# Attention and gated MLP on one core: a gather taken earlier in the gate, and a measurement of weights made one projection later

## The chip, the cores and the metric

The kernel runs on one core of a Trainium2 chip. The core's engines work side by side and are tied together by semaphores: TensorE (matrix products, which it writes to PSUM), VectorE, ScalarE, GpSimd, and SyncE, which only issues DMAs. In the profile they are called PE, DVE, ACT, POOL and SP; PEld is TensorE's loading of weights, and a name with q is the engine's queue. Each engine executes its own instructions in the order in which they were written. The metric is the device time of one execution in microseconds (us), lower is better.

## The reference, cut to what matters

The inputs are `x` (1 × 2048 × 512) and weights, all float32. Two blocks follow each other, each with a normalisation ahead and the input added behind:

```python
h  = x + attention(layernorm(x))        # 32 heads of 16, softmax over all 2048 keys, then @ wo
z  = gelu(layernorm(h) @ w_in)          # 2048 x 1376
z1 = z[:, :688]
z2 = layernorm(z[:, 688:])
g  = w_sp @ z2 + b_sp[:, None]          # w_sp is 2048 x 2048: it mixes the positions
h2 = h + (z1 * g) @ w_out               # what is returned
```

## The kernel before, in words

Every product of float32 numbers is made of three products of 16-bit numbers. Each operand is scaled by a power of two and split into a high and a low part, and `mm3` (L107 to L109) adds high × high, high × low and low × high in one PSUM accumulator. The scales are found on the chip, from the weights themselves.

The work has four stages: a prologue that normalises `x` and makes queries, keys and values (span to about 162 us); attention (to about 1295 us); a middle stage with `wo` and `w_in` (to about 1460 us); and the gate with `w_sp` and `w_out`. In all four the order on each engine is written out by hand (`tc.manual_schedule`): an instruction stands in its engine's queue where the Python code emits it. So the place of a line in the code is the place in five queues at once, and an instruction that waits holds up everything that was emitted after it for the same engine.

**Prologue.** The 512 columns of queries and of keys come in four blocks `b` of 128. For each block, `load_wqk(b)` reads the weights, `weigh_wqk(b)` takes the largest magnitude of each row of both (VectorE, L352) and spreads it over a diagonal matrix `each` (GpSimd, L356). The measurement proper, `measure(b, each)`, multiplies a matrix of ones with `each` on TensorE (L374), so that all partitions hold the maxima, and VectorE reduces them (L376) and makes powers of two of them (L299, L300, L302, L378). `weigh_wqk` doesn't call it, it appends it to the list `measures`, and the main code pops it later. `put_wqk(b)` then scales and splits the weights on GpSimd (L366, L100, L104). `proj` and `proj_qk` are the projections: 12 matmuls in four groups `d`; between the groups stand calls of `between(d)`, which take over the result of the projection before (`takes`: ScalarE L458, VectorE L461, or L492 for values), and, for the first two blocks of keys, two copies by ScalarE for sums of keys (L472, L473). There are three accumulators for projections. The measurement of the fourth block stood behind `proj(proj_v, 15)`, the last projection of values. Then a loop over `j` makes the 24 projections of blocks 1 to 3; from `j` = 2 on, `ahead` puts products for the row maxima of the scores among them (L223 on TensorE, L228 on VectorE). `put_wqk(2)` stands at `j` = 1, `put_wqk(3)` at `j` = 8. The last results are taken over by VectorE (L460, L461), then attention begins (L1112).

**Gate.** `w_sp` is taken as 2 × 2 blocks, with Strassen-like sums of blocks that were prepared before, so that seven block products take the place of eight. The loop over `p` handles a pair of row blocks, `p` and `p + 8`, eight times. `product(acc, b)` is one such product, 24 matmuls of 344 columns, and a `ring` of nine tiles brings the operands by DMA. The seven go to three accumulators A, C and B in the order `b11`, `t1`, `t2`, `b22`, `t3`, `b21`, `n4`. The results times `z1` are the tile `now.pr`: `right` (L1504 VectorE, L1505 GpSimd), `br` (L1512, L1513), `left` (L1522, L1523) and `bl` (L1540). Its columns are dealt with in two halves, 1 and 0. `level(half)` finds a power of two for each row (VectorE L1355, L1317 to L1320), `raise_` multiplies with it (ScalarE L1366), `squares` transposes blocks of 32 × 32 on VectorE (L1382 and L1385 for half 1, L1388 for half 0), and after half 0 `send` moves the blocks with 16 DMAs (SP L1395). In the next pair, whose name for this one is `before`, `hi` (ScalarE L1401) and `lo` (VectorE L1410, L1414, L1416) split them, `multiply(half, w)` multiplies them with `w_out` on TensorE, and `gather(half, w, acc)` adds the result to the rows of `h` (VectorE L1455). The accumulators of `multiply` come from the pool `ps_o`, which has two buffers. So `multiply(1, 0)` and `multiply(1, 1)` (8 matmuls of 512 columns each; L107 to L109, L1449, L1450) fill both, and `multiply(0, 0)` and `multiply(0, 1)` (9 matmuls each) need them back from the first and the second gather.

The last pair has no `squares`; its own columns are transposed on TensorE (L1426) instead.

Of the kernel before, what the change touches and what calls it, by code (L numbers as in the profile page):

```python
# [59 lines left out]
def block_kernel(ctx: ExitStack, tc: tile.TileContext, x, wqkv, wo, w_in, w_sp4, b_sp, w_out, out):  # L60
# [194 lines left out]
    def max_rows():  # L255

        g, parts = turned.pop(0)
        t = sm.tile([P, 32], F16, name="mturned")
        nc.vector.transpose(t, parts.rearrange("p t j i -> p (t j i)"))
        nc.sync.dma_start(m_scr[g % 2], t)  # L260
        for j in range(2):
            r0 = RG * j + KS
            nc.sync.dma_start(
                qst[g][r0:r0 + 2].rearrange("r p (c n s) -> r (p c) n s", n=4, s=32),
                m_scr[g % 2].rearrange("(n j r q) s -> j r q n s", n=4, j=2, r=2)[j])
# [3 lines left out]
    with ExitStack() as pre:  # L269
# [244 lines left out]
        kf, accs, rest, measures = {}, [0], [], []  # L514
# [17 lines left out]
        def ahead(k):  # L532
            for _ in range(k):
                m = done[0] // 8
                if not todo and m < LEAD:
                    steps = max_pair(m)
                    todo.extend(steps[i] for i in (0, 1, 4, 2, 5, 3, 6, 7))
                    ends.append(steps[8])
                if todo:
                    todo.pop(0)(done[0] % 5)  # L540
                    done[0] += 1
                    if not todo:
                        ends.pop()()
# [4 lines left out]
        def proj(kind, *which, then=lambda: None, **kw):  # L548

            def between(d):  # L550
                if d == 0 and rest:
                    rest.pop(0)()
                if d == 1:
                    if takes:
                        takes.pop(0)()
                    then()

            takes.append(kind(*which, between, **kw))
# [103 lines left out]
        measures.pop(0)()  # L662
        weigh_wqk(3)
        proj(proj_v, 15)
        measures.pop(0)()

        for j in range(24):
            b, n, i = 1 + j // 8, j // 2 % 4, 1 - j % 2

            def between(d):  # L670
                if d == 1 and j >= FIRST:
                    ahead(5 if j < FIRST + 4 else 4)
                if d == 2 and takes:
                    takes.pop(0)()
                    if rest:
                        rest.pop(0)()
                if d == 3 and turned and done[0] % 8 > 3:
                    max_rows()

            if j in (1, 8):  # L680
                put_wqk(2 + j // 8)
            if j == 3:
                copy_v = load_v(0)
            if j == 7:
                copy_v()
            if j in (8, 12):
                load_q(j // 4 - 1)
            if j == 16:
                fixed(kst[0])
            if j == 20:  # L690
                scales_ = [nc.scalar.alloc_register(f"scale{b}") for b in range(DB)]
                for reg, size in zip(scales_, sizes):
                    nc.scalar.load(reg, size[0:1, 3:4].bitcast(I32))
            takes.append(proj_qk(b, n, i, between))
# [91 lines left out]
    with ExitStack() as at:  # L786
# [13 lines left out]
        def product(s, hg, qb, kb, p, t):  # L800

            r = slice(RG * t, RG * t + KM)
            nc.tensor.matmul(s, kst[hg % 2][r, p, kb * P:(kb + 1) * P],  # L803
                             qst[hg * NQ + qb][r, p, :], start=True, stop=True)
# [484 lines left out]
    with ExitStack() as fin:  # L1289
# [9 lines left out]
        def next_g():  # L1299
            banks[0] += 1  # L1300
            return ps_g[(banks[0] - 1) // 2 % 2].tile([P, 512], F32, name="g")[:, :FC]
# [170 lines left out]
        with tc.manual_schedule(engines={E.PE, E.Activation, E.DVE, E.Pool, E.SP}):  # L1472
            wu = [f1.tile([P, 2 * 3, D], F16, name=f"wu{i}") for i in range(2)]
            raw_w = f1.tile([P, 2 * 3, D], F32, name="raw_w")
            w_top, w_low, w_up, w_down = [f1.tile([P, n], F32, name=f"w_{i}") for i, n in enumerate((6, 1, 1, 1))]
            nc.gpsimd.memset(raw_w[:, 2 * 3 - 1, :], 0.0)
            nc.sync.dma_start(raw_w[:, :5, :], w_out[:5 * P, :].rearrange("(i p) c -> p i c", p=P))
            for r0 in (TW - fn, P - fn):
                nc.sync.dma_start(raw_w[r0:r0 + fn, 5, :], w_out[5 * P:, :])
            nxt = fetch(0)  # L1480
            now = None
            for p in range(HB):
                (z1t, z1b, ht, hb), last = nxt, p + 1 == HB
                nxt = None if last else fetch(p + 1)
                before, now = now, Rows(p, (ht, hb))
                bt, bb = bias_up[:, p:p + 1], bias_up[:, p + HB:p + HB + 1]
                A, C, B = [next_g() for _ in range(3)]
                p1, v, q5 = [f0.tile([P, FC], F32, name=n) for n in ("p1", "v", "q5")]
                left, right = now.pr[:, 0, :FC], now.pr[:, 0, FC:FH]
                bl, br = now.pr[:, 1, :FC], now.pr[:, 1, FC:FH]  # L1490

                product(A, "b11")
                nc.scalar.activation(p1, A, AF.Identity, bias=bt)
                product(C, "t1")
                nc.scalar.activation(q5, C, AF.Identity, bias=bb)
                if not p:
                    weigh_w()
                product(A, "t2", False)
                nc.scalar.activation(v, A, AF.Identity, bias=bt)
                if p:  # L1500
                    before.lower(1, 0, 1)
                    before.lower(0, 0, 1)
                product(C, "b22", False)
                nc.vector.tensor_add(right, C, v)  # L1504
                nc.gpsimd.tensor_mul(right, right, z1t[:, FC:])  # L1505
                if p:
                    before.hi(1)
                    before.hi(0)
                else:
                    measure_w()  # L1510
                product(A, "t3", False)
                nc.vector.tensor_add(br, A, q5)  # L1512
                (nc.vector if last else nc.gpsimd).tensor_mul(br, br, z1b[:, FC:])  # L1513
                if p:
                    before.lo(1)
                    before.lo(0)
                now.level(1, 0, 1)
                now.raise_(1, 0, 1)
                if not last:
                    now.squares(1)  # L1520
                product(B, "b21")
                nc.vector.tensor_add(left, B, p1)  # L1522
                (nc.vector if last else nc.gpsimd).tensor_mul(left, left, z1t[:, :FC])  # L1523
                if p:
                    accs = [before.multiply(1, w) for w in range(2)]
                    for w in range(2):
                        before.gather(1, w, accs[w])
                if last:
                    now.level(0, 0)
                    for w in range(2):  # L1530
                        now.turn(1, w)
                        now.split(1, w)
                    now.lower(1, 0, 1)
                    now.raise_(0, 0)
                if p:
                    accs = [before.multiply(0, w) for w in range(2)]
                    for w in range(2):
                        before.gather(0, w, accs[w])
                product(A, "n4", False)
                nc.vector.scalar_tensor_tensor(bl, A, bb, z1b[:, :FC], op0=ALU.add, op1=ALU.mult)  # L1540
                if p:
                    for w in range(2):
                        before.store(w)
                if last:
                    now.level(0, 1)
                    now.raise_(0, 1)
                else:
                    now.level(0, 0, 1)
                    now.raise_(0, 0, 1)
                    now.squares(0)  # L1550
                    now.send()
            accs = [now.multiply(1, 0)]
            now.turn(0, 0)
            now.split(0, 0)
            accs.append(now.multiply(1, 1))
            now.turn(0, 1)
            now.gather(1, 0, accs[0])
            now.split(0, 1)
            now.gather(1, 1, accs[1])
            now.lower(0, 0, 1)  # L1560
            acc = now.multiply(0, 0)
            now.gather(0, 0, acc)
            now.store(0)
            acc = now.multiply(0, 1)
            for c in (slice(0, D // 2), slice(D // 2, D)):
                now.gather(0, 1, acc, c)
                now.store(1, c)
# [29 lines left out]
```

## Time and profile before

| | |
|---|---|
| median of 3 runs | 1720.6 us (1720.13 to 1721.52) |
| the profiled execution | 1720.39 us |
| its span, first to last instruction | 1718.6 us |
| granted clock of TensorE | 1.00 |
| TensorE busy | 1699.9 us, 99% |
| VectorE busy | 1452.8 us, 85% |
| ScalarE busy | 1317.3 us, 77% |
| GpSimd busy | 813.8 us, 47% |

All times of the trace count from the start of the span. A row of the timeline has the start, the duration, the engine, the line, the operation, output and inputs with their shapes, and how many like instructions are merged in it; in square brackets stands the idle time of the engine just before it and what ended that. A matmul's duration reaches to the end of its write, so that rows of matmuls in a stream overlap: the distance of two starts says how fast TensorE goes. A row of the waits has the instruction that waited, what it waited for, the total in us, how often, and the longest. A row of the chain that ended last has start, duration, engine, tile and line.

### The profile page before, as it was taken

How to read it: one execution, taken by the hardware profiler on the slowest of the kernel's cores; microseconds unless marked ns; L12 is line 12 of the kernel's file. 1: busy time of each engine (PE TensorE's matmuls, PEld its weight loads, DVE VectorE, ACT ScalarE, POOL GpSimd, SP SyncE). 2: the span in 40 equal slices, each digit the busy share in tenths (PEclk: the TensorE clock that was granted, in tenths of full speed). 3: DMA queues.
4: the chain of work that ended last, by engine and by line, in shares of the span. 5: the costliest groups of instructions: out<-in, count | busy, mean ns of one | idle time of the engine just before them, and what ended most of it. 6: DMA issues, size and time to landing. Idle time of an engine off the chain costs nothing.

```text
span 1718.6 us, 36670 instructions
## 1 busy us (share of the span) xinstructions
PE 1699.9 (99%) x13499; PEld 643.9 (37%) x13499; DVE 1452.8 (85%) x3051; ACT 1317.3 (77%) x2584; POOL 813.8 (47%) x1062
## 2 busy tenths in 40 slices
PE   9999999999999999999999999999999999999999
PEld 4533222222222222222222222222225666666655
DVE  7688999999999999999999999999937887533444
ACT  4334999999999999999999999999995554211111
POOL 1231867776673267687677876400002766200100
PEclk9999999999999999999999999999999999999999
DMA  5534332332221244344434444300114454654651
GB/s 183 163 99 134 111 88 64 105 94 81 81 67 25 55 118 117 110 145 123 124 112 139 129 129 126 80 13 19 45 41 125 146 183 143 241 193 159 211 199 44
DMA packets 189309, 196.03 MB, mean 114 GB/s; under 512 B 67496, under 2 KB 140008, under 8 KB 189128
## 3 DMA queue, kind: packets, MB, share of 16 engines
q1 hardware_dynamic: 186824, 188.04, 36.7%
q10 hardware_dynamic: 2304, 5.64, 0.8%
q8 instruction: 106, 1.74, 0.4%
q14 instruction: 75, 0.61, 0.1%
HBM read 122.10 MB, written 65.93 MB: 109 GB/s over the span
## 4 chain that ended last, share of the span: by engine, by line
PE 65%; DVE 16%; DMA 5%; issue 5%; SPq 4%; POOL 3%; ACT 2%; DVEq 0%; ACTq 0%; POOLq 0%
PE pv L828 26%; PE s L803 17%; PE m L223 9%; DVE mx L228 7%; PE acc L107 3%; PE acc L109 3%; PE acc L108 3%; SPq L1395 2%; DMA rc<-r_scr 2%; DVE ab L237 1%; DMA z_scr<-z 1%; DVE og L838 1%; PE g L108 1%; PE g L109 1%; PE g L107 1%
## 5 line engine op out<-in xcount | busy, mean ns | idle before, releaser
L812 ACT ACTIVATE pt<-s 128x512 f32<-128x512 f32 x1968 | 1006.2, 637 | 4.9 <-PE m L223 3.8
L228 DVE TENSOR_REDUCE mx<-m 128x1 f32<-128x512 f32 x1510 | 947.5, 682 | 12.6 <-PE m L223 3.9
L803 PE MATMUL s<-qst,kst 50*128 50x512 f16 x2048 | 604.3, 379 | 0.2
L828 PE MATMUL pv<-pt,vst 128*32 128x256 f32 (+1 forms) x6056 | 598.1, 466 | 4.1 <-DVE og L838 1.3
L223 PE MATMUL m<-kst,qst 48*128 48x512 f16 x1510 | 452.5, 381 | 0.0
L803 PEld LDWEIGHTS <-kst 50*128 50x128 f16 x2048 | 132.0, 94 | 352.0 <-issue 323.7
L828 PEld LDWEIGHTS pv<-pt,vst 128*32 128x32 f32 x6056 | 119.5, 108 | 290.1 <-issue 276.7
L223 PEld LDWEIGHTS <-qst 48*128 48x128 f16 x2048 | 159.1, 93 | 173.7 <-issue 124.3
L223 PE MATMUL m<-uvs,qst 48*128 48x512 f16 x504 | 190.5, 380 | 0.0
L245 POOL TENSOR_SCALAR nm<-nm 128x16 f32<-128x16 f32 x32 | 6.6, 206 | 359.0 <-DVE nm L242 359.0
L237 DVE CUSTOM_DVE_ANT_0 ab<-m,ab 128x512 f32<-128x512 f32 x252 | 170.5, 677 | 2.7 <-ACT ab L233 2.7
L233 ACT ACTIVATE ab<-m 128x512 f32<-128x512 f32 x252 | 157.3, 624 | 16.5 <-PE m L223 15.8
L1366 ACT ACTIVATE pr<-pr,up 128x304 f32<-128x304 f32 (+1 forms) x32 | 17.0, 574 | 114.8 <-DVE up L1320 110.5
L989 POOL TENSOR_TENSOR op<-raw,op 128x512 f16<-128x512 f32 x80 | 92.9, 1161 | 6.0
L912 POOL TENSOR_TENSOR raw<-raw 128x512 f32<-128x512 f32 (+1 forms) x84 | 83.3, 991 | 6.7
L917 POOL TENSOR_TENSOR acc_sp<-acc_sp,raw 128x512 f32<-128x512 f32 x63 | 80.4, 1277 | 4.5
L109 PE MATMUL acc<-wi,hT 128*128 128x344 f16 x256 | 79.1, 309 | 0.3 <-DVE hT L104 0.3
L107 PE MATMUL acc<-wi,hT 128*128 128x344 f16 x256 | 79.1, 309 | 0.0
L108 PE MATMUL acc<-wi,hT 128*128 128x344 f16 x256 | 79.1, 309 | 0.0
L1505 POOL TENSOR_TENSOR pr<-pr,z 128x344 f32<-128x344 f32 x8 | 7.3, 912 | 146.0 <-DMA whole<-squares 110.1
L909 POOL TENSOR_SCALAR raw<-raw 128x512 f32<-128x512 f32 (+1 forms) x88 | 52.3, 594 | 19.7 <-DMA raw<-in_wqkv 12.3
L894 POOL TENSOR_SCALAR raw<-raw,figs 128x512 f32<-128x512 f32 (+1 forms) x84 | 55.8, 668 | 8.8 <-DMA raw<-in_wo 7.9
(247 smaller groups left out, 2238.7 us busy)
## 6 DMA issues: line engine op xcount, KB each, us to landing
raw<-in_w_sp SPq DMA_DIRECT2D x128, 256.0 KB
s_scr<-op SPq DMA_DIRECT2D x64, 256.0 KB
op<-s_scr SPq DMA_DIRECT2D x32, 512.0 KB
a_scr<-op SPq DMA_DIRECT2D x48, 256.0 KB
op<-a_scr SPq DMA_DIRECT2D x24, 512.0 KB
o_scr<-og SPq DMA_DIRECT2D x64, 128.0 KB
qst<-q_scr SPq DMA_DIRECT2D x192, 32.0 KB
kst<-k_scr SPq DMA_DIRECT2D x48, 128.0 KB
```

What stands on the lines that cost most here:

```text
L107: nc.tensor.matmul(ps, lh, rh, start=first, stop=False, **kw)
L108: nc.tensor.matmul(ps, lh, rl, start=False, stop=False, **kw)
L109: nc.tensor.matmul(ps, ll, rh, start=False, stop=last, **kw)
L223: nc.tensor.matmul(acc, q[r, p, c], keys[r, p], start=True, stop=True)
L228: nc.vector.reduce_max(at(t, e if t else e - 1), acc, axis=AX.X)
L233: nc.scalar.activation(ab[0], acc, AF.Abs)
L237: nc.vector.tensor_tensor_reduce(ab[0], acc, ab[0], 0.5, LOW, ALU.add, ALU.max, at(0, 0))
L803: nc.tensor.matmul(s, kst[hg % 2][r, p, kb * P:(kb + 1) * P], qst[hg * NQ + qb][r, p, :], start=True, stop=True)
L812: nc.scalar.activation(pts[p, kb][:, t, :], s, AF.Exp, scale=scales_[hg // 2])
L828: nc.tensor.matmul(pv[0][32 * j:32 * j + 32, a:b], vst[hg % 2][:, c:c + 32], pts[j % 2, kb][:, j // 2, a:b], start=kb == 0, stop=kb == NB - 1,
L912: pool.tensor_mul(got[0] if n else acc, got[0], got[0])
L989: chores.append((lambda: pool.tensor_sub(t[0][:, 1], of(), t[0][:, 0]), TT))
```

## The change

Two edits. In the prologue, the fourth measurement is popped at `j` = 1 of the loop, behind the first of the 24 projections and ahead of `put_wqk(2)`; it stood ahead of that projection. In the gate, for a pair after the first, the two products `multiply(1, 0)` and `multiply(1, 1)` stand directly behind `b21`, and the first gather stands ahead of the sum into `left` (L1522) and of GpSimd's product; the second gather stays behind them. The transposes of half 1 (`now.squares(1)`), which stood ahead of `b21`, stand behind the second gather. TensorE's own order in the gate is the same as before. No instruction is added or taken away.

```diff
@@ prologue @@
         weigh_wqk(3)
         proj(proj_v, 15)
-        measures.pop(0)()
 
         for j in range(24):
...
+            if j == 1:
+                measures.pop(0)()
             if j in (1, 8):
                 put_wqk(2 + j // 8)
@@ gate @@
                 now.level(1, 0, 1)
                 now.raise_(1, 0, 1)
-                if not last:
-                    now.squares(1)
                 product(B, "b21")
+                if p:
+                    accs = [before.multiply(1, w) for w in range(2)]
+                    before.gather(1, 0, accs[0])
                 nc.vector.tensor_add(left, B, p1)
                 (nc.vector if last else nc.gpsimd).tensor_mul(left, left, z1t[:, :FC])
                 if p:
-                    accs = [before.multiply(1, w) for w in range(2)]
-                    for w in range(2):
-                        before.gather(1, w, accs[w])
+                    before.gather(1, 1, accs[1])
+                if not last:
+                    now.squares(1)
                 if last:
                     now.level(0, 0)
```

## The prediction

> **What bounds the kernel now.** I read four views in this order: the page's busy table, TensorE's waits over the whole span, the table of stages, and then the instructions in order of time around the two places that the diff touches.
>
> ```profile
> PE 1699.9 (99%) x13499; PEld 643.9 (37%) x13499; DVE 1452.8 (85%) x3051; ACT 1317.3 (77%) x2584; POOL 813.8 (47%) x1062
> ...
> PE acc L107 <- DVE h L1455: 5.0, 6, 1.0
> PE m L374 <- POOL each L356: 0.7, 1, 0.7
> ...
> 250.00:600.00 350.00, 348.50 (x3158) 98.90 (x3151) 347.49 (x682) 349.39 (x711) 209.69 (x281) 1.00 0.27 71
> ...
> 1566.00:1599.00 33.00, 32.23 (x205) 19.87 (x204) 13.19 (x30) 5.52 (x10) 2.87 (x3) 1.00 0.53 187
> ```
>
> The first row says that TensorE is busy 99% of the span: what shortens the kernel is time in which TensorE stands still. The next two (engine, line, what it waited for, us in total, times, longest) are the waits that the two edits aim at: six waits on the gather of L1455, 5.0 us, and one on the products of L356, 0.7 us. In the stage rows (TensorE, weight loads, VectorE, ScalarE, GpSimd, then the clock, DMA share and GB/s) TensorE falls 0.77 us short of full in a gate pair of about 33 us. Attention (250 to 600) has TensorE, VectorE and ScalarE all above 99%: its length is given by its own work, so an earlier start moves it as a whole.
>
> **The gate edit.** In each pair after the first, `before.multiply(1, 0)` and `multiply(1, 1)` fill both buffers of the output accumulator. The next product, `multiply(0, 0)`, needs the first one back, so it waits until VectorE has done the first gather. In pair 3:
>
> ```profile
> 1563.78 0.38 PE L107 MATMUL acc<-wu,pT 128*128 128x512 f16 x1
> ...
> 1565.29 0.38 PE L1450 MATMUL acc<-wu,pT 128*128 128x512 f16 x1
> 1565.51 0.38 PE L107 MATMUL acc<-wu,pT 128*128 128x512 f16 x1
> ...
> 1567.02 0.38 PE L1450 MATMUL acc<-wu,pT 128*128 128x512 f16 x1
> 1568.16 0.38 PE L107 MATMUL acc<-wu,pT 128*128 128x512 f16 x1 [0.77 <-DVE h L1455]
> ...
> 1569.89 0.38 PE L109 MATMUL acc<-wu,pT 128*128 128x512 f16 x1
> ...
> 1562.39 0.42 DVE L1416 TENSOR_TENSOR pT<-whole,pT 64x256 f16<-64x256 f32 x1
> ...
> 1564.94 0.17 DVE L1320 TENSOR_SCALAR up<-low 128x2 int32<-128x2 int32 x1
> 1565.79 0.88 DVE L1382 STREAM_TRANSPOSE squares<-pr 128x256 f32<-128x256 f32 x2 [0.68 <-ACT pr L1366]
> 1566.59 0.46 DVE L1385 STREAM_TRANSPOSE squares<-pr 128x128 f32<-128x128 f32 x2
> 1566.98 0.48 DVE L1522 TENSOR_TENSOR pr<-g,p 128x344 f32<-128x344 f32 x1
> 1567.38 1.39 DVE L1455 SCALAR_TENSOR_TENSOR h<-acc,low,h 128x512 f32<-128x512 f32 x2
> 1570.31 0.75 DVE L1455 SCALAR_TENSOR_TENSOR h<-acc,low,h 128x512 f32<-128x512 f32 x1 [1.54 <-PE acc L109]
> 1572.25 0.75 DVE L1455 SCALAR_TENSOR_TENSOR h<-acc,low,h 128x512 f32<-128x512 f32 x1 [1.19 <-PE acc L109]
> 1575.75 0.58 DVE L1540 SCALAR_TENSOR_TENSOR pr<-g,fig,z 128x344 f32<-128x344 f32 x1 [2.75 <-PE g L109]
> ```
>
> The first accumulator is complete when the matmul of 1565.29 ends (1565.67). VectorE is then waiting 0.68 us for ScalarE's raise, does four transposes (1565.79 to 1566.98) and the sum of L1522, and takes the first gather only at 1567.38. TensorE, ready long before, resumes at 1568.16, some 0.78 us after that start.
>
> *New order.* VectorE is free at about 1565.15, after the L1320 of 1564.94. The gather of 1570.31 starts 0.42 us after the start of the last matmul that it waits for (1569.89), so the moved gather starts at 1565.29 + 0.42 = 1565.71. With the same 0.78 us the accumulator is back at 1566.49. Back to back, TensorE starts a matmul every 0.216 us (1565.29 to 1565.51) and would want it at 1567.02 + 0.216 = 1567.24. It comes 0.75 us early, and the wait is gone.
>
> *What that is worth.* Not only the idle column. A matmul's row is 0.38 us long while the next starts after 0.216 us, so a standstill also loses the overlap, 0.38 − 0.216 = 0.164 us. From start to start the gap is 1.14 us where 0.22 would do: 0.92 us saved. Over the six waits: 5.0 + 6 × 0.164 = **6.0 us**. [...]
>
> *What is late next.* The sum of L1522 follows the gather (about 1566.4 to 1566.85), earlier than the 1566.98 of today, and GpSimd's product behind it starts earlier too. The second gather starts when the second accumulator is full, 1567.02 + 0.42 = 1567.44, and ends by 1568.2; `multiply(0, 1)` wants its buffer at 1567.24 + 9 × 0.216 = 1569.18, so 0.99 us are to spare. The moved transposes take 1.19 us from 1568.15 to 1569.35. The gather behind them can start at 1567.24 + 8 × 0.216 + 0.42 = 1569.39: they fit into the 1.54 us in which VectorE now idles there, and even if they did not, the 2.75 us of idle before L1540 come next. Nothing reads the squares before the DMAs after the half-0 squares, which follow L1540. Their 16 issues on SP and landing, ScalarE's copies and VectorE's subtractions all run between the end of `n4` and the next pair's `multiply(1, 0)`, a stretch out of which no TensorE time is taken: this chain is not tightened.
>
> *First and last pair.* Pair 0 has no gather; its sum and transposes only change places, both ahead of L1540 as before, so that L1540 and what follows start no later: 0. In pair 7 there are no transposes:
>
> ```profile
> 1696.72 0.22 PE acc L1450
> ...
> 1697.10 0.75 DVE L1455 SCALAR_TENSOR_TENSOR h<-acc,low,h 128x512 f32<-128x512 f32 x1
> 1698.71 0.75 DVE L1455 SCALAR_TENSOR_TENSOR h<-acc,low,h 128x512 f32<-128x512 f32 x1 [0.86 <-PE acc L1450]
> ...
> 1703.25 0.75 DVE L1455 SCALAR_TENSOR_TENSOR h<-acc,low,h 128x512 f32<-128x512 f32 x1 [0.25 <-PE acc L109]
> ```
>
> The gather goes ahead of the sum and its product, but can't start before 1696.72 + 0.42 = 1697.14, as today; sum and product then fill the 0.86 us of idle. At most 0.2 us of delay reach the ops behind, and the 0.25 us of idle before 1703.25 takes them. I count 0.
>
> **The prologue edit.** It moves one small TensorE product (two matmuls, L374) and the five small VectorE operations on its result behind the next projection. No DMA and no GpSimd instruction is in it.
>
> ```profile
> 80.75 0.59 PE L374 MATMUL m<-each,every 128*128 128x256 f32 x2
> 81.18 0.38 PE L107 MATMUL acc<-wv,xT 128*128 128x512 f16 x1
> ...
> 83.55 0.38 PE L109 MATMUL acc<-wv,xT 128*128 128x512 f16 x1
> 84.66 0.70 PE L374 MATMUL m<-each,every 128*128 128x256 f32 x2 [0.73 <-POOL each L356]
> 85.19 0.38 PE L107 MATMUL acc<-xT,wqk 128*128 128x512 f16 x1
> ...
> 83.88 0.72 POOL L356 TENSOR_SCALAR each<-ident,most 128x128 f32<-128x128 f32 x2 [4.79 <-DVE most L352]
> 88.62 1.16 POOL L104 TENSOR_TENSOR wqk<-wg,wqk 128x512 f16<-128x512 f32 x1
> ...
> 85.85 0.17 DVE L299 TENSOR_SCALAR low<-low 128x2 f32<-128x2 f32 x1
> 86.06 1.16 DVE L300 TENSOR_SCALAR low<-low 128x2 int32<-128x2 int32 x1
> ...
> 88.61 0.69 DVE L461 SCALAR_TENSOR_TENSOR part<-acc,part 128x512 f16<-128x512 f32 x1
> ```
>
> Today TensorE starts nothing from 83.55 to 84.66; back to back it would be 83.77. The product then takes 0.53 us to the next start (84.66 to 85.19), where the unstalled one took 0.43 (80.75 to 81.18). Behind the projection it comes 12 × 0.216 = 2.6 us later, at 86.36, when its operand (84.6) is long there. Saved: 0.89 + 0.10 = **1.0 us**.
>
> What must hide the move: VectorE's chain now starts at about 87.0 and ends between 88.1 (each small step 0.2 us) and 90.1 (held up by GpSimd's work until 88.62 + 1.16 = 89.78, as L300 was stretched from 0.17 to 1.16 us). Behind it on VectorE stands L461 of that projection (0.69 us, so to 90.8 at the worst), behind that two ScalarE copies of the same accumulator:
>
> ```profile
> 89.34 0.59 ACT L472 ACTIVATE kf<-acc 64x512 f32<-64x512 f32 x1 [0.76 <-DVE part L461]
> ...
> 91.77 0.60 PE L223 MATMUL m<-kst,qst 48*128 48x512 f16 x3
> 93.82 0.38 PE L107 MATMUL acc<-xT,wqk 128*128 128x512 f16 x1
> ...
> 162.32 0.69 DVE L460 TENSOR_SCALAR part<-acc 128x512 f16<-128x512 f32 x1 [0.50 <-PE acc L109]
> 163.88 1.06 PE L1112 MATMUL pv<-vst 128*32 128x512 f32 x8 [0.84 <-DVE part L461]
> ```
>
> At the worst they end at 92.0. The accumulator is wanted by the projection that starts at 93.82 now and at 92.83 then: 0.8 us to spare. The scaling figure itself is wanted only by `put_wqk(3)`, seven projections on. The rest of the prologue is TensorE's (at 162.32 VectorE still waits for it), so attention starts 1.0 us earlier.
>
> **Sum.** 6.0 + 1.0 = 7.0 us. The profiled execution took 1720.39 us (span 1718.6), 0.2 below the median of 1720.6. Predicted: span 1711.6, profiled time 1713.4, median **1713.6 us**, −0.41%. A measurement here tells about 0.2% (3.4 us) from no change.
>
> **The rivals.**
> *A. Only part of the sum arrives: 1714.6 to 1715.6.* Either edit's last microsecond is lost: the gate is worth its idle column alone (5.0), or the prologue's gain is given back. The second hangs on VectorE's small steps being held up longer than 0.8 us past my worst case. [...] The moved steps meet the same GpSimd sequence, which ends at 89.78 whatever VectorE does, so I gave the worst case its full length.
> *B. The gate edit doesn't do what it says: 1719.6.* If the moved gather were released only with the second accumulator (1567.44 instead of 1565.71), TensorE would resume at 1568.22, as today, and only the prologue's 1.0 us would come. Against it: in pair 7 the gather of 1697.10 starts 0.38 us after the first accumulator's last matmul, while the second one's products run.
> *C. Slower: VectorE becomes late behind the gathers, about 1727.* The transposes, now between the second and the third gather, delay L1540 and with it level, raise, squares, the 16 SP issues, landing and the next `multiply(1, 0)`. This decides only when VectorE is late by more than the 1.19 + 2.75 = 3.94 us of idle before 1572.25 and 1575.75 and the 0.97 us from the subtraction's end (1562.39 + 0.42) to `multiply(1, 0)` at 1563.78. Each further us costs 1 us in six pairs; 2.2 us more would give −7.0 + 13.2 = +6.2 us. The transposes are 1.19 us in all, and even stretched by 1 us each, as L300 was, they use 4.0 us more: within the cover of 4.9.
>
> **How the numbers follow.** Forecast 0.66, A 0.20, B 0.08, C 0.06. Forecast and A are faster by over 0.2%, B is no change, C is slower: faster 0.86, same 0.08, slower 0.06. The range takes the forecast and A, with the spread of the runs shown (1720.13 to 1721.52) on both sides: 1712.4 to 1716.4.
>
> **What would show it.** Right: no wait of TensorE on L1455 in pairs 1 to 6, pairs 0.9 us shorter, gathers ahead of L1522, transposes directly behind the second gather; in the prologue L374 without idle before it and the first L223 at 90.8. Wrong: a wait of `multiply(0, 1)`, a new wait of `multiply(1, 0)` on VectorE, or L1112 still at 163.9.

## The result, and the profile after

The changed kernel takes **1713.2 us** (median of 6 runs, 1712.8 to 1715.04) against 1720.49 us before (6 runs, 1720.13 to 1721.52): 7.3 us less, ratio 0.9958 with a 95% interval of 0.9948 to 0.9968. The profiled execution took 1713.42 us, its span is 1711.6 us. Forecast were 1713.6, 1713.4 and 1711.6.

Behind the edits the lines of the code have moved by one to four: L1455 (gather) is L1456 now, L1522 (sum) L1524, L1540 L1542, L1320 L1321, L1382 and L1385 (transposes) L1383 and L1386, L1450 L1451, L1112 L1113.

TensorE's waits over the whole span of the changed kernel, longest total first (engine, line, what it waited for; us in total, times, longest):

```profile
PE pv L829 <- DVE og L839: 1.3, 6, 0.3
PE m L308 <- ACT junk L295: 1.3, 1, 1.3
PE acc L526 <- DVE idle L520: 1.2, 1, 1.2
PE pv L1113 <- DVE part L461: 0.8, 1, 0.8
```

The two rows that stood for the edits, 5.0 us on the gather and 0.7 us on the products for the measurement, are gone, and nothing has come in their place. The timeline of pair 3, TensorE:

```profile
1562.26 0.38 PE L1451 MATMUL acc<-wu,pT 128*128 128x512 f16 x1
1562.47 0.38 PE L107 MATMUL acc<-wu,pT 128*128 128x512 f16 x1
...
1563.98 0.38 PE L1451 MATMUL acc<-wu,pT 128*128 128x512 f16 x1
1564.20 0.38 PE L107 MATMUL acc<-wu,pT 128*128 128x512 f16 x1
```

From the start of the last matmul of `multiply(1, 1)` (1563.98) to that of the first matmul of `multiply(0, 0)` (1564.20) there are 0.22 us now, one ordinary step; they were 1.14 us. The same pair on VectorE:

```profile
1561.91 0.17 DVE L1321 TENSOR_SCALAR up<-low 128x2 int32<-128x2 int32 x1
1562.67 0.75 DVE L1456 SCALAR_TENSOR_TENSOR h<-acc,low,h 128x512 f32<-128x512 f32 x1 [0.60 <-PE acc L1451]
1563.34 0.51 DVE L1524 TENSOR_TENSOR pr<-g,p 128x344 f32<-128x344 f32 x1
1564.40 0.75 DVE L1456 SCALAR_TENSOR_TENSOR h<-acc,low,h 128x512 f32<-128x512 f32 x1 [0.56 <-PE acc L1451]
1565.07 0.76 DVE L1383 STREAM_TRANSPOSE squares<-pr 128x256 f32<-128x256 f32 x2
1565.76 0.46 DVE L1386 STREAM_TRANSPOSE squares<-pr 128x128 f32<-128x128 f32 x2
1566.35 0.75 DVE L1456 SCALAR_TENSOR_TENSOR h<-acc,low,h 128x512 f32<-128x512 f32 x1
1568.29 0.75 DVE L1456 SCALAR_TENSOR_TENSOR h<-acc,low,h 128x512 f32<-128x512 f32 x1 [1.19 <-PE acc L109]
1571.79 0.58 DVE L1542 SCALAR_TENSOR_TENSOR pr<-g,fig,z 128x344 f32<-128x344 f32 x1 [2.75 <-PE g L109]
```

VectorE now waits for TensorE ahead of both first gathers (0.60 and 0.56 us): that is the sign that its queue no longer decides. The transposes lie in what was idle time behind the second gather, and the third gather follows them without a gap; the 2.75 us ahead of L1542 are untouched. The prologue, TensorE's and VectorE's timeline around the moved measurement and the first product of attention:

```profile
85.78 0.60 PE L374 MATMUL m<-each,every 128*128 128x256 f32 x2
90.19 0.60 PE L223 MATMUL m<-kst,qst 48*128 48x512 f16 x3
...
162.30 1.07 PE L1113 MATMUL pv<-vst 128*32 128x512 f32 x8 [0.84 <-DVE part L461]
...
86.87 0.42 DVE L299 TENSOR_SCALAR low<-low 128x2 f32<-128x2 f32 x1
87.33 0.17 DVE L300 TENSOR_SCALAR low<-low 128x2 int32<-128x2 int32 x1
87.53 0.46 DVE L302 TENSOR_SCALAR size<-low 128x2 int32<-128x2 int32 x1
...
88.03 0.67 DVE L461 SCALAR_TENSOR_TENSOR part<-acc,part 128x512 f16<-128x512 f32 x1
```

L374 has no idle time before it, and the 0.84 us at the start of attention stayed, only earlier.

**Where the 7.0 us of the span came from.** I cut both traces at the same instructions (starts on TensorE: the last matmul of the last projection of values, the first L223, L1112, the first matmul of the middle stage with `w_in`, the first of the gate). For the gate's start, before:

```profile
1452.12 0.31 PE L107 MATMUL g<-b,op 128*128 128x344 f16 x1
```

and after:

```profile
1451.21 0.31 PE L107 MATMUL g<-b,op 128*128 128x344 f16 x1
```

| stretch | before, us | after, us | difference |
|---|---|---|---|
| start to the last projection of values | 83.55 | 82.98 | −0.57 |
| from there to the first L223 (the prologue edit) | 8.22 | 7.21 | −1.01 |
| to the start of attention | 72.11 | 72.11 | 0.00 |
| attention, to the first matmul with `w_in` | 1134.53 | 1134.47 | −0.06 |
| middle stage | 153.71 | 154.44 | +0.73 |
| gate (the gate edit) | 266.48 | 260.39 | −6.09 |

The two edited stretches give 7.1 us. The first stretch and the middle stage hold no edit. In the 14 profiles of this study they lie between 82.88 and 83.75 us and between 153.01 and 154.69 us, so −0.57 and +0.73 are what one execution differs from another. That they almost cancel here, and that the span was met to 0.1 us, is luck.

### The profile page after: what moved, and what is told of

Read it like the earlier page. It is cut to its first block, busy times and chain, and to the rows that moved or that the text cites. A ratio compares the mean times of both kernels' runs of the same rounds, so it can differ in the third digit from the quotient of the medians.

```text
span 1711.6 us, 36671 instructions
## 1 busy us (share of the span) xinstructions
PE 1699.2 (99%) x13499; PEld 643.8 (38%) x13499; DVE 1452.3 (85%) x3051; ACT 1317.3 (77%) x2584; POOL 811.9 (47%) x1062
## 4 chain that ended last, share of the span: by engine, by line
PE 77%; DVE 13%; DMA 3%; POOL 3%; SPq 2%; ACT 1%; issue 1%; DVEq 0%; ACTq 0%; POOLq 0%
PE pv L829 26%; PE s L804 17%; PE m L223 9%; DVE mx L228 7%; PE g L108 4%; PE g L109 4%; PE g L107 4%; PE acc L107 4%; PE acc L109 3%; PE acc L108 3%; DMA rc<-r_scr 2%; DVE ab L237 1%; DVE og L839 1%; SPq L722 1%; DMA raw<-in_w_sp 1%
## 5 line engine op out<-in xcount | busy, mean ns | idle before, releaser
L223 PE MATMUL m<-kst,qst 48*128 48x512 f16 x1510 | 452.3, 381 | 0.0
L223 PEld LDWEIGHTS <-qst 48*128 48x128 f16 x2048 | 159.3, 93 | 174.2 <-issue 124.6
L223 PE MATMUL m<-uvs,qst 48*128 48x512 f16 x504 | 190.7, 380 | 0.0
L1505 DVE TENSOR_TENSOR pr<-g,v 128x344 f32<-128x344 f32 x8 | 4.1, 516 | 66.6 <-PE g L109 63.5
```

Of the source, the lines that this page charges most:

```text
L223: nc.tensor.matmul(acc, q[r, p, c], keys[r, p], start=True, stop=True)
```

## The experiments

All times below are medians of 5 to 11 runs, beside the kernel before on the same chip; the two columns on the right are read from the one profiled execution of each kernel.

| kernel | median, us | before, us | difference | gate, us | to the first L223, us |
|---|---|---|---|---|---|
| e1_prologue_only | 1719.88 | 1720.80 | −0.9 | 266.40 | 7.22 |
| e2_gate_only | 1714.37 | 1720.80 | −6.4 | 260.39 | 8.20 |
| e3_gather_only | 1718.77 | 1720.80 | −2.0 | 264.01 | 8.21 |
| e4_squares_only | 1714.58 | 1720.80 | −6.2 | 260.44 | 8.21 |
| e5_ahead2 | 1713.98 | 1721.03 | −7.1 | 260.67 | 7.22 |
| e6_ahead4 | 1722.03 | 1721.03 | +1.0 | 268.87 | 7.22 |
| e7_behind6 | 1713.53 | 1721.03 | −7.5 | 260.42 | 7.22 |
| e8_behind12 | 1726.00 | 1721.03 | +5.0 | 272.30 | 7.22 |
| e9_three_acc | 1717.42 | 1720.92 | −3.5 | 264.42 | 8.22 |
| e10_weigh_early | 1719.41 | 1720.92 | −1.5 | 266.65 | 7.22 |
| e11_ahead6 | 1734.71 | 1720.99 | +13.7 | 282.57 | 7.21 |
| e12_three_acc_bank | 1714.77 | 1720.99 | −6.2 | 260.28 | 8.21 |

My theory was that the six waits belong to the return of one of two accumulators, that VectorE's queue ahead of the first gather sets their length, and that the prologue's wait is for its operand. The rivals were that the two edits need each other, that both halves of the gate edit have a share, and that the late transposes cost something behind.

### e1_prologue_only and e2_gate_only: one edit each

e1 takes over the first part of the diff and nothing of the second, e2 the second and nothing of the first.

> The kernel before with the prologue edit alone. Theory (TensorE bounds the prologue and attention moves as a whole): L374 without idle before it, attention (L1113) 1.0 us earlier from the edit, the six gate waits on L1455 still there with 5.0 us; time 1.0 us less than before, or as little as 0.2 us if the middle stage, whose input DMAs landed 0.8 us later against its start in the profile of the changed kernel, swallows it. Rival (the prologue is bound by VectorE or by a DMA): attention no earlier, time as before.

> The kernel before with the gate edit alone. Theory: no wait on L1455 in pairs 1 to 6, pairs 0.92 to 1.16 us shorter, 6.0 us less than before; L374 still waits 0.7 us. Rival (the gate is worth its idle column alone): 5.0 us less. Rival (two edits need each other): clearly less than 5.

In e1 TensorE's waits still have the gate's row:

```profile
PE acc L107 <- DVE h L1456: 5.1, 6, 1.0
```

L374 waits no longer and its stretch is 1.0 us shorter. In the time this is 0.9 us (ratio 0.9995, 0.9986 to 1.0004), which by itself can't be told from no change; the stretch can. e2 has the whole gain of the gate, 6.1 us by the stretch and 6.4 by the time (0.9962, 0.9948 to 0.9976). The edits add up and don't need each other, and the gate is worth more than its idle column of 5.0 us.

### e3_gather_only and e4_squares_only: the two halves of the gate edit

```diff
# e3: only the first gather goes ahead of the sum
                 product(B, "b21")
+                if p:
+                    accs = [before.multiply(1, w) for w in range(2)]
+                    before.gather(1, 0, accs[0])
                 nc.vector.tensor_add(left, B, p1)
...
# e4: only the transposes go behind both gathers
-                if not last:
-                    now.squares(1)
                 product(B, "b21")
...
                         before.gather(1, w, accs[w])
+                if not last:
+                    now.squares(1)
```

> The kernel before with one half of the gate edit: the first gather goes ahead of the sum into left, but the transposes stay ahead of b21, and so ahead of the gather. Theory (VectorE's queue ahead of the first gather sets when TensorE resumes): the gather starts where the sum of L1522 starts today, 0.40 us earlier; TensorE still waits in six pairs, 0.37 us each by the idle column instead of 0.83; 0.40 x 6 = 2.4 us less than before. Rival (the order of gather and sum is what counts): nearly 6.0 us less.

> The kernel before with the other half of the gate edit: the transposes go behind the second gather, the sum into left stays ahead of both gathers. Theory: VectorE is free 0.85 us earlier at the sum, the sum ends (0.45 us) at about the time at which the first accumulator is full, so the first gather starts no later than 0.05 us after it does in the full edit; no wait of TensorE is left; 6.0 us less than before: this half alone is the whole gain, and the gather ahead of the sum adds nothing. Rival (both halves are needed, each with its share of 1.19 and 0.40 us): 3.6 us less.

e3: a wait of 0.45 us on average is left in six pairs,

```profile
PE acc L107 <- DVE h L1455: 2.7, 6, 0.6
```

and the gate is 2.5 us shorter. e4: no such row, and the gate is 6.0 us shorter, with the sum (L1520 there) ahead of the gather (L1455):

```profile
1563.46 0.51 DVE L1520 TENSOR_TENSOR pr<-g,p 128x344 f32<-128x344 f32 x1
1564.14 0.75 DVE L1455 SCALAR_TENSOR_TENSOR h<-acc,low,h 128x512 f32<-128x512 f32 x1 [0.18 <-PE acc L1450]
```

Even behind the sum the gather waits 0.18 us for TensorE. So **the transposes alone make the difference**; the part of the diff that the title names, the gather ahead of the sum, is worth 2.5 us alone and adds nothing once the transposes are out of the way.

### e5_ahead2 and e6_ahead4: how much room the new order has ahead of the gather

```diff
                     accs = [before.multiply(1, w) for w in range(2)]
+                    if not last:
+                        for _ in range(2):          # e6: 4, e11: 6
+                            nc.vector.reduce_max(spare, raw_w[:, 0, :], axis=AX.X)
                     before.gather(1, 0, accs[0])
```

> The changed kernel with two extra reductions (0.60 us each in a stream) on VectorE just ahead of the first gather in pairs 1 to 6; their result is used by nothing. Theory: VectorE stood idle 0.56 us there and the accumulator came back 0.75 us before TensorE wanted it, 1.31 us of cover together against 1.2 us of work: no wait of TensorE of more than 0.1 us, time as the changed kernel's. Rival (TensorE resumes later for every us that VectorE is late, as in the kernel before): 7.2 us more than the changed kernel.

> The same with four extra reductions, 2.4 us in pairs 1 to 6. Theory: 2.4 - 1.31 = 1.09 us a pair come through, TensorE waits on the gather again, 6.5 us more than the changed kernel, so about the time of the kernel before. Rival (another wait binds behind it): clearly more than 6.5 us; (the cover is larger): clearly less.

Two extra reductions cost nothing that can be told (gate +0.3 us). Four cost 8.5 us (gate 268.87 against 260.39). The timeline of pair 3 and the row of the waits of e6 show why that is more than 6.5:

```profile
1564.50 2.84 DVE L1526 TENSOR_REDUCE spare<-raw_w 128x1 f32<-128x512 f32 x4
1567.26 0.74 DVE L1456 SCALAR_TENSOR_TENSOR h<-acc,low,h 128x512 f32<-128x512 f32 x1
...
1568.05 0.38 PE L107 MATMUL acc<-wu,pT 128*128 128x512 f16 x1 [1.18 <-DVE h L1456]
```

```profile
PE acc L107 <- DVE h L1456: 7.5, 6, 1.4
```

The four took 2.76 us (1564.50 to 1567.26), 0.69 each and not the 0.60 I had reckoned. 2.76 − 1.31 = 1.45 us a pair is 8.7 us, and 8.5 came. The waits' 7.5 and six times the lost overlap of 0.164 us make 8.5 too. The cover of 1.31 us holds, and the 1.45 us beyond it on VectorE came through on TensorE as 1.42 us a pair (8.5 / 6).

### e7_behind6 and e8_behind12: how much room there is behind it

```diff
                 if not last:
                     now.squares(1)
+                if p and not last:
+                    for _ in range(6):              # e8: 12
+                        nc.vector.reduce_max(spare, raw_w[:, 0, :], axis=AX.X)
```

> The changed kernel with six extra reductions (3.6 us) on VectorE behind the moved transposes in pairs 1 to 6. Theory: the place behind the second gather has 3.9 us of idle VectorE time ahead of L1542 and 0.97 us ahead of the next multiply(1, 0), 4.9 us together: no cost, time as the changed kernel's. Rival (work behind the gathers delays the accumulators of multiply(0, 0) and (0, 1) or the stores): up to 3.6 us a pair, 21 us more.

> The same with twelve extra reductions, 7.2 us in pairs 1 to 6. Theory (rival C of the prediction, made to happen): 7.2 - 4.9 = 2.3 us a pair, TensorE waits at the next pair's multiply(1, 0) for the subtractions of L1415 to L1417, 13.8 us more than the changed kernel. If the 0.97 us are no cover: 19.6 us more. If this chain never binds: as the changed kernel.

Six cost nothing (gate 260.42), twelve 11.9 us. But TensorE did not wait where I had put it. The waits of e8, and then its timeline in pair 3, VectorE and TensorE:

```profile
PE g L107 <- DVE pr L1546: 4.1, 3, 1.4
PE g L107 <- ACT p L1495: 3.6, 3, 1.2
```

```profile
1572.23 8.57 DVE L1533 TENSOR_REDUCE spare<-raw_w 128x1 f32<-128x512 f32 x12
1580.72 1.40 DVE L1456 SCALAR_TENSOR_TENSOR h<-acc,low,h 128x512 f32<-128x512 f32 x2
1582.04 0.57 DVE L1546 SCALAR_TENSOR_TENSOR pr<-g,fig,z 128x344 f32<-128x344 f32 x1
...
1582.66 0.31 PE L107 MATMUL g<-t,op 128*128 128x344 f16 x1 [1.40 <-DVE pr L1546]
```

The late L1546 (L1540 of before) still reads accumulator A when the next pair's second product, `t1`, wants its bank, and in the other three pairs ScalarE, late with the raise that hangs on VectorE's level, holds up L1495, which has to read the next pair's A before the third product, `t2`, adds to it. That happens ahead of `multiply(1, 0)`, where only a wait of 0.2 us on ScalarE's copies is left; 1.1 us in all are waited on the gather behind it. The work was also larger, 8.5 us (1572.23 to 1580.72). 8.5 us gave 2.0 us a pair (11.9 / 6), so the cover is about 6.5 us, not 4.9.

### e10_weigh_early: the measurement in its old place, its operand earlier

```diff
         weigh_wqk(2)
+        weigh_wqk(3)
         proj(proj_v, 14)
         load_k(0)
         measures.pop(0)()
-        weigh_wqk(3)
         proj(proj_v, 15)
         measures.pop(0)()
```

> The kernel before with the fourth measurement in its old place, but its two reductions and the products of L356 made one projection earlier, directly behind those of the third. Theory (the wait is for the operand, and the place matters only through it): L374 without idle before it, attention 1.0 us earlier, time as with the prologue edit alone. Rival (what counts is that the measurement stands away from the last projection of values): L374 waits as before, time as before.

The stretch is 7.22 us, as with the edit, and L374 has no idle before it; the time is 1.5 us less (0.9993, 0.9984 to 1.0002), which by itself can't be told from no change; as with e1 the stretch decides. The operand is what TensorE waited for; the place is one of two ways round it.

### e9_three_acc and e12_three_acc_bank: a third accumulator instead of another order

```diff
# e9 (the kernel before, pools alone)
-        ps_t = fin.enter_context(tc.tile_pool(name="fin_t", bufs=2, space=PSUM))
-        ps_o = fin.enter_context(tc.tile_pool(name="fin_o", bufs=2, space=PSUM))
+        ps_t = fin.enter_context(tc.tile_pool(name="fin_t", bufs=1, space=PSUM))
+        ps_o = fin.enter_context(tc.tile_pool(name="fin_o", bufs=3, space=PSUM))
# e12: e9, and in turn(), for the second tile of the last pair
-                tp = self.turned[half, w] = ps_t.tile([P, 512], F32, name="tp").rearrange(
+                banks[0] += w
+                own = ps_g[(banks[0] - 1) // 2 % 2].tile([P, 512], F32, name="g") if w else \
+                    ps_t.tile([P, 512], F32, name="tp")
+                tp = self.turned[half, w] = own.rearrange(
```

e9 keeps the order of before; the output accumulators have three buffers, the transposes on TensorE one instead of two.

> [...] Theory (the wait is for the return of one of two accumulators, not for the gather's result): multiply(0, 0) has a free buffer and the six waits on L1455 go, 6.0 us less; in the last pair the second transpose waits for the single buffer, about 2.1 us more; together 3.9 us less than before. Rival (multiply(0, 0) waits for VectorE for another reason, its subtractions for instance): the waits stay, 2.1 us more than before.

> The kernel with the old order and three accumulators again, but the second transposed tile of the last pair goes to a bank of the gate's accumulators that is free by then, so that it waits for nothing. Theory: with the wait of 2.27 us and the slow clock behind it gone (4.0 us together), the whole 6.0 us of the six gate waits remain as gain, as with the gate edit. Rival (a part of the 4.0 us came from the third buffer itself): 2 to 4 us less than before.

In e9 the six waits on L1455 are gone with VectorE's order unchanged, so the buffer is their cause. But in the profiled execution the gate is only 2.1 us shorter, not 3.9. Its end shows the expected wait and something that I had not expected. TensorE's wait, three rows of its timeline, and the table of stages (TensorE, weight loads, VectorE, ScalarE, GpSimd, then the granted clock):

```profile
PE tp L1426 <- DVE pT L1438: 2.3, 1, 2.3
```

```profile
1695.72 0.87 PE L1426 MATMUL tp<-ident,pr 128*128 128x128 f32 x3 [2.27 <-DVE pT L1438]
1696.39 0.63 PE L107 MATMUL acc<-wu,pT 128*128 128x512 f16 x1
1696.82 0.63 PE L108 MATMUL acc<-wu,pT 128*128 128x512 f16 x1
```

```profile
1697.00:1699.00 2.00, 2.00 (x7) 0.66 (x5) 1.05 (x4) 0.63 (x2) 0.00 (x0) 0.50 0.00 0
```

Behind this standstill of 2.27 us the clock was 0.50 (1697 to 1699 us), and matmuls of 512 columns started 0.43 us apart instead of 0.216. That took another 1.6 us or so. By the mean clock it did not come in every execution: in five of e9's eleven, the profiled one among them, the mean clock was 0.999 and the median 1718.66 us (2.3 less than before); in the other six it was 1.000 and the median 1717.26 us (3.7 less, close to the 3.9 expected). With the wait removed, e12 has the gate at 260.28 us: **the whole gain of the gate edit without a change of order** (0.9966, 0.9952 to 0.9979).

### e11_ahead6: is it the standstill that lowers the clock?

> The changed kernel with six extra reductions ahead of the first gather in pairs 1 to 6. They took 0.69 us each with four of them, so 4.14 us, less 1.31 us of cover: TensorE stands still 2.8 us more in each of six pairs. Theory (a standstill of TensorE of over 2 us also lowers the granted clock, as behind the 2.27 us wait of the kernel with three accumulators, where the clock was 0.5 for 2 us and matmuls started every 0.43 us): about 1.6 us more for each, 6 x (2.8 + 1.6) = 26 us more than the changed kernel, and a clock below 1 behind each wait. Rival (the low clock there belongs to the transposes or to the end of the kernel): clock 1.00 in the pairs and 17 us more.

The gate took 282.57 us, 22.2 more than the changed kernel's, between the two numbers. The waits, and the stages behind those of pairs 1, 2 and 3:

```profile
PE acc L107 <- DVE h L1456: 16.1, 6, 2.8
```

```profile
1503.00:1509.00 6.00, 5.75 (x20) 2.32 (x20) 3.09 (x8) 0.00 (x0) 0.92 (x1) 0.72 0.58 232
1539.00:1545.00 6.00, 5.44 (x29) 2.83 (x29) 4.15 (x9) 0.00 (x0) 0.91 (x1) 1.00 0.67 264
1574.00:1580.00 6.00, 5.82 (x20) 2.37 (x20) 3.07 (x9) 0.00 (x0) 0.92 (x1) 0.72 0.45 178
```

The waits took 16.1 us in six pairs, 2.7 us on average and 2.8 us at the longest, yet the clock fell behind those of pairs 1 and 3 (0.72 in these 6 us) and stayed at 1.00 behind that of pair 2. 16.1 + 6 × 0.164 = 17.1 us are standstill, and 22.2 − 17.1 = 5.1 us are left; by the 1.6 us or so of e9 that is, as an estimate, three falls of the clock in the six pairs. So the fall is not bound to the transposes or the end of the kernel, and a standstill of this length was followed by it in some pairs and not in others; what decides it, these views do not show. By the mean clock it also differs between executions: three of e11's five had 0.997 and 1734.71 to 1736.29 us, two had 0.999 and 1731.78 and 1732.43 us.

## Why the prediction was right, step by step

- *TensorE bounds the kernel, and attention moves as a whole.* Right. The prologue's 1.0 us is there at the first L223 and, with 72.11 us in between, at the start of attention; attention kept its length to 0.1 us.
- *The moved gather starts 0.42 us after the first accumulator's last matmul.* 1562.26 to 1562.67: 0.41 us. VectorE's idle ahead of it was put at 0.56 us and was 0.60.
- *The gate is worth 6.0 us, not the 5.0 of the idle column.* Right: 6.1 us by the stretch, and e2, e4 and e12 agree (260.39, 260.44, 260.28 us). The first matmul of `n4`, a pair's last product with `w_sp`, came earlier against before by 1.16, 0.92, 0.93, 0.96, 1.10 and 0.93 us more in pairs 1 to 6, 6.0 us together.
- *What is late next.* Right that nothing is: the second gather (1564.40) had 0.56 us to wait for its operand, and the transposes just fit ahead of the third gather, which follows them at once. e5 confirms the 1.31 us of cover ahead of the gather.
- *The prologue edit is worth 1.0 us and is hidden.* Right, 1.01. The small steps on VectorE took less than in my worst case (0.42 us for L299, 0.17 before, and 0.46 for L302, 0.64 before; each ended within 0.02 us of the GpSimd instruction that ran beside it, L366 and L100, as the 1.16 us of L300 before ended within 0.03 us of L104). That GpSimd's work holds such a step up is my reading of these ends. GpSimd's own rows beside them kept their lengths (0.69, 0.61 to 0.63 and 1.16 us). L461 started at 88.03; with the 0.57 us of the earlier start added, 1.5 us ahead of that case.
- *First and last pair cost nothing.* Right for TensorE: by the same measure, pair 0 gained less than 0.1 us and pair 7 nothing. On VectorE L1542 of pair 0 even came 0.4 us earlier within the gate, since the sum fills a wait for ScalarE's raise (0.75 us before, 0.34 us of it left).
- *Rivals A and B.* Neither edit lost a part of its worth; and the first gather starts at 1562.67, while the second accumulator's products run until 1564, so it isn't released with the second accumulator.
- *Rival C, transposes that make VectorE late.* It did not happen, and its mechanism stood in the wrong place: e8 shows that the first thing a late VectorE holds up is the next pair's `t1` and `t2` (banks that L1540 and L1495 must have read), not `multiply(1, 0)`, and that the cover is about 6.5 us, not 4.9.
- What the prediction did not know is that a standstill of 2.27 us (e9) or 2.7 us on average (e11) can cost more than itself, 1.6 us or so. At the lengths in question (1.0 us at most in the kernel before) the clock stayed at 1.00, so no term was touched.

## What to carry to other kernels

A wait of the bounding engine is removed by letting the releasing instruction start earlier or by making the buffer it waits for unnecessary. Three ways were measured here: other work moved behind the releasing instruction (e4, 6.0 us of the gate), an earlier operand (e10, 1.0 us of the prologue) and a third buffer (e12, 6.2 us of the gate). Look which item of the queue ahead of it is the long one, since here moving the 1.19 us of transposes was enough, and moving the gather past the 0.4 us of the sum alone brought 2.5 of the 6 us. Price a removed wait from start to start, not by the idle column: here TensorE lost 0.164 us more at each of them, a sixth of the gain. And count how far the moved work may slip before someone else waits, by the buffers that its successors free and not only by the data that they make.

## What the runs showed of the hardware

Standstills of TensorE of at most 1.0 us (six in the gate of the kernel before) and 1.4 us (e6) left the granted clock at 1.00. Behind the standstill of 2.27 us in e9 the clock was 0.50 from 1697 to 1699 us, and a matmul of 512 columns started every 0.43 us instead of 0.216; that cost 1.6 us or so. In e11, with six standstills of 2.7 us on average, the clock was 0.72 over 6 us behind those of pairs 1 and 3 and 1.00 behind that of pair 2, and 5.1 us more than the standstills were lost. The same kernel did not lose the same in every execution: the mean clock was 0.999 in five of e9's eleven and 1.000 in six, and 0.997 in three of e11's five and 0.999 in two. What decides whether a standstill of such a length is followed by a lower clock was not shown.
